# Zero blocks copied within DRAM instead of stored from SBUF, with the freed SBUF holding an eleventh weight chunk

## Chip, cores, metric

One core of a Trainium2 chip. The metric is device time in microseconds (us) of one execution. A run counts as slow when it lies more than 1.5% above the fastest run of the same kernel; verdicts use the fast runs alone.

## The reference, cut to what matters

A decode step of two attention layers (A) and two MLP layers (B), forward and backward. The outputs are the result and the gradients of all inputs and weights but one.

```python
def _A_ref(x, k_cache, v_cache, wq, wo):         # D=1024, 32 heads of 128, 4 groups, Sk=32768
    W = min(4096, max(256, Sk // 4))             # only the last 4096 positions are attended to
    k = k_cache[:, :, Sk - W:, :]; v = v_cache[:, :, Sk - W:, :]
    ...
    return o @ wo
x = x + A(norm(x)); x = x + B(norm(x)); x = x + A(norm(x)); x = x + B(norm(x))
_out, _vjp = jax.vjp(...)                        # out_2, out_3: gradients of k_cache and v_cache
```

The gradients of the two caches, out_2 and out_3, are zero at the first 28,672 of 32,768 positions of each group. These zeros are 58.7 MB, and the kernel has to write them.

## The kernel before

A tile of zeros in SBUF (4 KB per partition) is stored 112 times, 128 rows of 4 KB each. Some of these stores go out on the SP queue. The others go out on the GpSimd queue behind a "gate": a tiny copy that reads a tile of the computation, so that the zeros start only when that tile is there.

```python
NB = 6                       # buffers of the ring "strm" for streamed weights
NR = 10                      # wo chunks kept in SBUF, of 16
...
strm = ctx.enter_context(tc.tile_pool(name="strm", bufs=NB))
...
ZC = 2048
zt = keep.tile([P, ZC], BF16, name="zt")
nc.gpsimd.memset(zt[:], 0.0)
# zero_jobs: 112 destinations of 128 rows x 4 KB in out_2 and out_3  (loop cut)
def zeros(n):
    for _ in range(min(n, len(zero_jobs))):
        nc.sync.dma_start(zero_jobs.pop(0), zt[:])
def bg_zeros(n, after):
    if n:
        nc.gpsimd.tensor_copy(gate_t[:], after[:, 0:1])
    for _ in range(min(n, len(zero_jobs))):
        nc.gpsimd.dma_start(zero_jobs.pop(0), zt[:])
...
def w1_load(i):              # wo_load and w2_load take ring buffers in the same way
    w = strm.tile([P, F // 2], BF16, name="w1_c", tag="st", padded_shape=[P, 2048])
    nc.sync.dma_start(w[:], w1_v[:, t, hf * (F // 2):(hf + 1) * (F // 2)])
    return w
...
def w1_T():                  # the last pass over w1: 16 streamed loads
    i, ws = w1s["n"], w1s["ws"]
    w = w1_load(i); ws[i] = w
    if i in Z["W1m"]:        # 2, 5, 8, 11, 13
        bg_zeros(1, ws[i - 1])          # the gate reads a ring buffer
    xpose(...)
...
zeros(Z["A1d"])              # 23 blocks on the SP queue, after the last attention stage's loads
```

Of the kernel before, what the change touches and what calls it, by code (L numbers as in the profile page):

```python
# [9 lines left out]
BF16 = mybir.dt.bfloat16  # L10
# [4 lines left out]
P = 128  # L15
# [1 line left out]
DH = 128  # L17
G = 4
NB = 6
NR = 10  # L20


@with_exitstack
def kernel(
# [22 lines left out]
    nc = tc.nc  # L47
# [20 lines left out]
    keep = ctx.enter_context(tc.tile_pool(name="keep", bufs=1))  # L68
# [44 lines left out]
    ident_f = keep.tile([P, P], FP32, name="ident_f")  # L113
    make_identity(nc, ident_f[:])
    nc.vector.tensor_add(sel2[:], ident_f[:, 0:P:64], ident_f[:, 32:P:64])
    ZC = 2048
    zt = keep.tile([P, ZC], BF16, name="zt")
    nc.gpsimd.memset(zt[:], 0.0)

    zero_jobs = []  # L120
    per = ZR // P * DH
    for out_t in (out_2, out_3):
        for g in range(G):
            zflat = out_t[0, g, 0:ZR, :].rearrange("(p r) d -> p (r d)", p=P)
            for i in range(per // ZC):
                zero_jobs.append(zflat[:, i * ZC:(i + 1) * ZC])

    def zeros(n):
        for _ in range(min(n, len(zero_jobs))):
            nc.sync.dma_start(zero_jobs.pop(0), zt[:])  # L130

    gate_t = keep.tile([P, 1], BF16, name="gate_t")

    def bg_zeros(n, after):

        if n:
            nc.gpsimd.tensor_copy(gate_t[:], after[:, 0:1])
        for _ in range(min(n, len(zero_jobs))):
            nc.gpsimd.dma_start(zero_jobs.pop(0), zt[:])  # L139

    ev = [0.0, 0.0]

# [191 lines left out]
    wq_t = [wq_b[:, t, hf, :] for t in range(TD) for hf in range(2)]  # L334
    wo_b = keep.tile([P, NR, 2, D], BF16, name="wo_b")
    wo_kept = {c: wo_b[:, c, :, :] for c in range(NR)}
    wo_rows = wo_b[:].rearrange("p c t d -> p (c t) d")

    def load_kv(pool, nm, src):
        kv[nm] = pool.tile([P, G, TK, DH], BF16, name=nm)  # L340
        for g in range(G):
            nc.sync.dma_start(kv[nm][:, g, :, :], src[g])
# [7 lines left out]
    def wo_load(c):  # L350
        if c < NR:
            w = wo_kept[c]
        else:
            w = strm.tile([P, 2, D], BF16, name="wo_c", tag="st")[:]
        nc.sync.dma_start(w, wo_v[c])
        return w
# [83 lines left out]
    def attn_fwd(x_col, lname, first):  # L440
        if first:
# [4 lines left out]
            load_kv(keep, "V", v_v)  # L446
            for c in range(NR):
                wo_load(c)
# [22 lines left out]
        if not first:  # L471
            for c in range(NR, min(NO, NR + NB)):
                held[c] = wo_load(c)
            bg_zeros(Z["A3"], n_bf)
            for w in wq_t:
                xq["wq"].extend(w[:, k * 1024:(k + 1) * 1024] for k in range(2))
            fill(1, ["wq"], "v")
# [69 lines left out]
        NRW = NO - 2 if first else NO - 3  # L547
        late, early = list(range(NR, NO)), list(range(NR))
        order = early + late if first else late[0:3] + early + late[3:]
# [62 lines left out]
    class W2Pass:  # L612
# [33 lines left out]
        def rest(self, done, g_bf, x_col, xname, gbc, zn, last=None):  # L646
            for c in range(NW2):
                w = self.get(c)
                if c >= done:
                    self.fwd(c)  # L650
                    self.tc(c)
                scr = work.tile([P, D], BF16, name="scr", tag="kp")
                nc.vector.tensor_tensor_reduce(out=scr[:], in0=w[:, 0, :], in1=gbc[:], scale=1.0, scalar=0.0,  # L653
                                               op0=ALU.mult, op1=ALU.add, accum_out=self.wg[:, c, 0:1])
                if c:
                    self.bwd(c - 1, g_bf)
                if c in zn:
                    bg_zeros(zn[c], self.wg[:, c, :])
            hook("w1")
            self.bwd(NW2 - 1, g_bf)  # L660
            hook("w1b")
            if last is not None:
                last()
            x_new = keep.tile([P, TD], FP32, name=xname)
            nc.vector.tensor_add(x_new[:], x_col[:], self.acc.cols(0, TD))
            nc.vector.tensor_copy(self.wg[:, :, 1:2], self.acc.cols(TD, TD + NW2)[:, :, None])
            return x_new, self.wg

    def mlp_fwd(x_col, lname, g_bf):
# [5 lines left out]
        for i in range(2 * TD):  # L675
            t, hf = i // 2, i % 2
            w = w1_load(i)
            if i == 0:
                bg_zeros(Z["B2a"], x_col)
            if i == 4:  # L680
                gbc = bcast_row(g_bf)
            for b in range(NW2):
                fb = hf * NW2 + b
                o = (b // 2) * 2 * P + b % 2
                mv(hacc, fb, w[:, o:o + 2 * P - 1:2], n_bf[:, t:t + 1], False, t == TD - 1)
# [131 lines left out]
    def attn_bwd(g_col, g_bf, lname, sv, first, nxt):  # L817
# [63 lines left out]
        if first:  # L881
            pre.extend(w2_load(c) for c in range(NB))
            bg_zeros(Z["A3d"], g_bf)
            fill(100, ["V"])
        else:
            after_stream()
            zeros(Z["A1d"])
# [406 lines left out]
    for at in (27, 33):  # L1294
        jobs.insert(at, lambda: zeros(2))
    run(1000)
    zeros(1000)
    assert not zero_jobs

# [29 lines left out]
```

## Time and profile before

| | before |
|---|---|
| median (range), first three runs | 442.62 us (442.41 to 445.55) |
| span of the profiled run | 439.8 us |
| packet time: all packet records added up, over 16 engines | 436.4 us |
| rest of the span | 3.3 us |

The packet time is the useful summary here. Added up, the packets take 436.4 of 439.8 us, so the kernel can only gain by moving fewer bytes or moving them faster, and it loses whatever makes the packets longer or leaves the engines empty. The two rows are a summary and not exact: packet records overlap a little (full stretches show a DMA share of 1.02 or 1.03 below), so the rest understates the time in which engines stand empty. Counted from the trace, as the share of the 16 engines with no packet under way at each moment, the empty time is 13.4 us.

The prediction shows the main rows of the page. In such rows each digit is the busy share, in tenths, of one of 40 equal slices of the span. PE is TensorE, PEld its weight loads, DVE VectorE, ACT ScalarE, POOL GpSimd, SP SyncE (a "q" marks the part that issues); L139 is line 139 of the kernel. One more row, the bytes moved in each of the 40 slices (11 us each):

```profile
GB/s 319 421 422 414 407 409 391 409 380 373 407 416 354 353 349 352 409 395 416 415 409 376 401 388 362 363 401 414 417 415 418 416 380 267 379 401 409 417 421 304
```

It stays near 410 wherever large blocks move, be they zeros or weights. The dips to 350 (slices 13 to 16) are stages with many small packets.

### The profile page before, as it was taken

To read this page: it belongs to the slowest core of one execution; us is meant where nothing else is said; L and a number is where in the kernel's file an instruction comes from. 1 tells how busy PE (TensorE), PEld (TensorE's weight loads), DVE (VectorE), ACT (ScalarE), POOL (GpSimd) and SP (SyncE) were. 2 spreads that over 40 slices of the span, in tenths; PEclk is the share of its full clock that TensorE was granted. 3 is DMA by queue.
4 is the path that set the end of the run, shared out by engine and by line. 5 is a ranking of instruction groups with operands and counts; after the bars stand their busy time and mean duration, and the time that the engine had idled before them with its cause. 6 is when DMAs were issued, how large, how long until landed. Compare 5 with 4: busy or idle time off the path is not lost.

```text
span 439.8 us, 11711 instructions
## 1 busy us (share of the span) xinstructions
PE 319.4 (73%) x5004; PEld 216.7 (49%) x5004; DVE 241.1 (55%) x494; ACT 219.4 (50%) x254; POOL 64.6 (15%) x168
## 2 busy tenths in 40 slices
PE   1566855597989988878897588777956688588830
PEld 0343525487467978866776588755421122211100
DVE  3134201186333757584357555365369889899930
ACT  1131200075153867666865243426047888798840
POOL 2000000011420322152332111214010010000000
PEclk9998565575879999998999558899975555555555
DMA  8999999999999999999999999999999996999997
GB/s 319 421 422 414 407 409 391 409 380 373 407 416 354 353 349 352 409 395 416 415 409 376 401 388 362 363 401 414 417 415 418 416 380 267 379 401 409 417 421 304
DMA packets 48721, 171.18 MB, mean 389 GB/s; under 512 B 4929, under 2 KB 12125, under 8 KB 44573
## 3 DMA queue, kind: packets, MB, share of 16 engines
q1 hardware_dynamic: 36208, 125.58, 72.8%
q0 software_dynamic: 12416, 44.84, 25.7%
q8 instruction: 39, 0.64, 0.5%
q14 instruction: 14, 0.11, 0.1%
q10 hardware_dynamic: 44, 0.01, 0.0%
HBM read 71.58 MB, written 98.84 MB: 388 GB/s over the span
## 4 chain that ended last, share of the span: by engine, by line
PE 24%; ACT 13%; DMA 10%; DVE 4%; issue 2%; POOL 1%; ACTq 0%; DVEq 0%; SPq 0%
DMA w_c<-in_B_w_dram 7%; PE tps L196 7%; PE ops L232 6%; PE acc L232 5%; ACT wq_b L149 3%; ACT K L149 3%; DMA out_dram<-wq_b 2%; ACT st_o L149 2%; PE sm L232 2%; ACT V L149 2%; ACT wo_b L149 2%; PE rw L995 1%; PE d L232 1%; PE tps L629 1%; PE wps L155 1%
## 5 line engine op out<-in xcount | busy, mean ns | idle before, releaser
L139 POOL DMA_DIRECT2D out_dram<-zt x85 | 45.6, 540 | 43.2 <-DMA out_dram<-zt 37.0
L232 PEld LDWEIGHTS <-w_c 128*128 128x128 bf16 x1120 | 37.9, 103 | 25.2 <-DMA w_c<-in_B_w_dram 19.0
L639 ACT COPY w_c<-tps 128x1024 bf16<-128x1024 bf16 x28 | 28.3, 1012 | 30.1 <-PE tps L629 22.4
L653 DVE CUSTOM_DVE_ANT_0 scr<-w_c,gbc 128x1024 bf16<-128x1024 bf16 x28 | 34.2, 1221 | 12.0 <-DMA w_c<-in_B_w_dram 10.8
L232 PE MATMUL ops<-V 2*128 2x512 bf16 (+1 forms) x160 | 33.4, 602 | 4.8 <-ACT V L149 1.2
L149 ACT CAST wq_b<-ops 128x1024 bf16<-128x1024 f32 (+1 forms) x33 | 35.9, 1126 | 1.9 <-PE ops L232 1.8
L146 DVE CAST wq_b<-ops 128x1024 bf16<-128x1024 f32 (+1 forms) x31 | 34.4, 1139 | 2.0 <-PE ops L232 1.6
L149 ACT COPY K<-tps 128x1024 bf16<-128x1024 bf16 x20 | 19.5, 1023 | 28.3 <-PE tps L196 28.2
L232 PEld LDWEIGHTS <-V 128*128 128x128 bf16 (+2 forms) x448 | 16.8, 102 | 33.7 <-issue 32.0
L232 PE MATMUL ops<-wo_b 2*128 2x512 bf16 x120 | 23.5, 553 | 10.0 <-ACT wq_b L149 2.8
L629 PE MATMUL tps<-ident_bf,w_c 128*128 128x128 bf16 x224 | 24.2, 275 | 0.7 <-DMA w_c<-in_B_w_dram 0.7
L232 PE MATMUL acc<-a_pair,w_c 128*128 128x16 bf16 x448 | 15.9, 173 | 9.5 <-DMA w_c<-in_B_w_dram 9.2
L149 ACT COPY w_b<-tps 128x1024 bf16<-128x1024 bf16 x20 | 19.5, 1015 | 5.3 <-PE tps L196 5.2
L196 PE MATMUL tps<-ident_bf,w_c 128*128 128x128 bf16 x224 | 19.0, 250 | 3.5 <-DMA w_c<-in_B_w_dram 3.4
L146 DVE COPY w_c<-tps 128x1024 bf16<-128x1024 bf16 (+1 forms) x20 | 12.7, 650 | 15.5 <-PE tps L196 13.4
L146 DVE COPY K<-tps 128x1024 bf16<-128x1024 bf16 x12 | 8.1, 689 | 23.6 <-PE tps L196 23.6
L232 PE MATMUL q<-wq_b,nA_pair 128*32 128x512 bf16 x128 | 9.5, 414 | 15.7 <-DMA wq_b<-in_A_wq_dram 15.7
L232 PEld LDWEIGHTS <-wo_b 2*128 2x128 bf16 (+1 forms) x184 | 7.4, 98 | 27.0 <-issue 24.7
L149 ACT CAST K<-ops 128x1024 bf16<-128x1024 f32 x17 | 17.1, 1012 | 6.3 <-PE ops L232 5.5
L196 PE MATMUL tps<-ident_bf,K 128*128 128x128 bf16 x256 | 20.0, 239 | 0.0
L146 DVE CAST K<-ops 128x1024 bf16<-128x1024 f32 x15 | 18.3, 1222 | 3.1 <-PE ops L232 2.7
L248 DVE COPY yr<-acc 128x512 f32<-128x512 f32 x6 | 4.2, 692 | 28.7 <-PE acc L232 28.7
(326 smaller groups left out, 657.5 us busy)
## 6 DMA issues: line engine op xcount, KB each, us to landing
out_dram<-zt POOLq DMA_DIRECT2D x85, 512.0 KB, 10.3
w_c<-in_B_w_dram SPq DMA_DIRECT2D x32, 448.0 KB, 6.7
w_c<-in_B_w_dram SPq DMA_DIRECT2D x28, 512.0 KB, 7.7
out_dram<-zt SPq DMA_DIRECT2D x27, 512.0 KB, 10.0
wo_c<-in_A_wo_dram SPq DMA_DIRECT2D x24, 512.0 KB, 8.3
wq_b<-in_A_wq_dram SPq DMA_DIRECT2D x8, 1024.0 KB, 21.1
out_dram<-K SPq DMA_DIRECT2D x8, 1024.0 KB, 9.6
out_dram<-wq_b SPq DMA_DIRECT2D x8, 1024.0 KB, 10.3
```

Of the source, the lines that this page charges most:

```text
L139: nc.gpsimd.dma_start(zero_jobs.pop(0), zt[:])
L146: nc.vector.tensor_copy(out_ap, in_ap)
L149: nc.scalar.copy(out_ap, in_ap)
L155: nc.tensor.matmul(ps, lhsT=ident_bf[:], rhs=ident_bf[:, None, :].to_broadcast([P, 4, P]), start=True, stop=True, skip_group_check=True)
L196: nc.tensor.transpose(ps[:, b, :], ap, ident_bf[:])
L232: nc.tensor.matmul(out_ap, lhsT=lhsT, rhs=rhs, start=start, stop=stop, skip_group_check=True, **kw)
L248: nc.vector.tensor_copy(yr[:], bank[:])
L629: nc.tensor.transpose(self.ps[c][:, b, :], w[:, 1, b * P:(b + 1) * P], ident_bf[:])
L639: nc.scalar.copy(self.w[c][:, 1, :], self.ps.pop(c)[:].rearrange("p b c -> p (b c)"))
L653: nc.vector.tensor_tensor_reduce(out=scr[:], in0=w[:, 0, :], in1=gbc[:], scale=1.0, scalar=0.0, op0=ALU.mult, op1=ALU.add, accum_out=self. ...
L995: nc.tensor.transpose(ps[:, j, :], sp[:, j, :], ident_bf[:])
```

## The change

Its intent: one zeroed block of out_2 becomes the source, and all other zero blocks are copied from it, from DRAM to DRAM, with rows of 8 KB instead of 4. The SBUF tile of zeros is no longer needed; its 4 KB per partition keep one more chunk of wo, which saves one 512 KB reload in each of three passes.

```diff
-NR = 10
+NR = 11
...
-    ZC = 2048
-    zt = keep.tile([P, ZC], BF16, name="zt")
-    nc.gpsimd.memset(zt[:], 0.0)
+    ZC = 4096
...
-                zero_jobs.append(zflat[:, i * ZC:(i + 1) * ZC])
+                for hp in range(2):
+                    zero_jobs.append(zflat[hp * 64:hp * 64 + 64, i * ZC:(i + 1) * ZC])
+    zsrc = zero_jobs[0]
+    def seed(tiles):
+        zero_jobs.pop(0)
+        for i, t in enumerate(tiles):
+            nc.gpsimd.memset(t[0:64, :], 0.0)
+            nc.gpsimd.dma_start(zsrc[:, i * 2048:(i + 1) * 2048], t[0:64, :])
...   (in zeros and in bg_zeros)
-            nc.sync.dma_start(zero_jobs.pop(0), zt[:])
+            nc.sync.dma_start(zero_jobs.pop(0), zsrc)
...
+    seed([wo_b[:, c, :, :].rearrange("p t d -> p (t d)") for c in (NR - 2, NR - 1)])
```

More of the change, by code (lines that the diff above doesn't have):

```diff
@@ L138, in bg_zeros @@
         for _ in range(min(n, len(zero_jobs))):
-            nc.gpsimd.dma_start(zero_jobs.pop(0), zt[:])
+            nc.gpsimd.dma_start(zero_jobs.pop(0), zsrc)
     ev = [0.0, 0.0]
```

## The prediction

> **What bounds the kernel now.** I first read the page's header, its 40 slices (11 us each), the HBM totals and the largest DMA groups.
>
> ```profile
> PE   1566855597989988878897588777956688588830
> DVE  3134201186333757584357555365369889899930
> DMA  8999999999999999999999999999999996999997
> HBM read 71.58 MB, written 98.84 MB: 388 GB/s over the span
> out_dram<-zt POOLq DMA_DIRECT2D x85, 512.0 KB, 10.3
> out_dram<-zt SPq DMA_DIRECT2D x27, 512.0 KB, 10.0
> wo_c<-in_A_wo_dram SPq DMA_DIRECT2D x24, 512.0 KB, 8.3
> ```
>
> The DMA row is 9 in all but four slices; no compute engine is near that before 320 us. 171 MB pass through the 16 DMA engines. Of these, 112 x 524,288 B = 58.7 MB are zeros for the parts of out_2 and out_3 outside the window: one third of all traffic. These are what the change touches.
>
> Next I asked for the busy time in stretches: two in which nearly nothing but zeros moves on the GpSimd queue, one with zeros on the SP queue, and the hole near the end.
>
> ```profile
> core 0: us, PE busy (x) PEld busy (x) DVE busy (x) ACT busy (x) POOL busy (x), PEclk, DMA share, GB/s
> 120.00:132.00 12.00, 9.92 (x224) 8.09 (x220) 5.10 (x16) 5.66 (x10) 3.20 (x6) 0.80 1.02 414
> 216.00:236.00 20.00, 19.73 (x351) 16.50 (x348) 11.85 (x22) 12.54 (x14) 7.71 (x14) 1.00 1.02 409
> 301.00:322.00 21.00, 18.18 (x253) 9.90 (x249) 7.45 (x20) 5.50 (x9) 1.56 (x10) 1.00 1.03 416
> 366.00:377.00 11.00, 8.77 (x60) 2.81 (x59) 10.71 (x17) 8.84 (x9) 0.00 (x0) 0.50 0.58 235
> ```
>
> Zeros alone keep the engines full at 409 to 416 GB/s. The only real hole is 366 to 377 us: 0.42 x 11 = about 5 us, where VectorE (10.71 of 11 us) sets the pace of the outputs. Only that much extra DMA time could hide.
>
> Last I followed the chain of work between 238 and 290 us.
>
> ```profile
> 240.61 10.60 DMA w_c<-in_B_w_dram
> 253.00 7.86 DMA w_c<-in_B_w_dram
> 272.20 7.44 DMA w_c<-in_B_w_dram
> 281.57 5.80 DMA w_c<-in_B_w_dram
> ```
>
> PE waits 6 to 11 us for weight loads right after a stretch of 28 zero blocks. Zeros aren't filling free time there: DMA time in front of a load is span. So I treat the kernel up to about 325 us as bound by the sum of DMA packet times, and the rest by VectorE, ScalarE and DMA in about equal parts.
>
> **What the Trainium skill says.**
> - "Perfetto Trace Analysis", DMA Optimizations: batching transfers into larger ones ("2KB → 4KB or 8KB") can help much. The trace agrees only weakly: its packet records have a median of 159 ns for 4096 B (zeros and loads alike) and 312 ns for 8192 B. Two small packets cost 318 ns, so 2% is to be had.
> - "HBM Reference", Specifications (TRN2): about 716 GB/s for the memory domain that two cores share. No run here shows this limit: the kernel never moves more than some 420 GB/s in reads plus writes.
> - "DMA: Bandwidth & Descriptors", Latency and other measured facts: copies of 128-row tiles between HBM tensors reach 207 to 214 GB/s "per direction" at harmless row pitches. The trace has no such copy, so it neither agrees nor disagrees. The page doesn't say if the copy was one DMA or passed through SBUF.
> - The same page, Queues, rings and completion order: an engine alternates between its queues packet by packet. The trace fits: in 200 to 215 us 4 KB zeros and 4 KB loads each have about half of the bytes.
>
> **The change part by part.**
>
> 1. *Reloads removed.* With 11 instead of 10 wo chunks kept, the first pass still loads 16; each of the three later passes reloads 5 instead of 6. Loads of wo fall from 34 to 31. One chunk is 524,288 / 4096 / 16 = 8 packets per engine, 8 x 159 ns = 1.27 us. Three are **-3.8 us**, all in DMA-bound stretches.
>
> 2. *Longer runs.* A zero block was 128 rows of 4 KB, 8 packets per engine, 1272 ns; it becomes 64 rows of 8 KB, 4 packets. If a packet from DRAM to DRAM costs what an 8 KB load or store does, a block takes 4 x 312 = 1248 ns. 111 x 24 ns = **-2.7 us**.
>
> 3. *Source moved from SBUF to HBM.* This is the term that decides. Every zero byte is now also read from HBM: 111 x 0.524 = 58.2 MB more reads, 129.8 - 1.6 = 128 MB in place of 71.6, and 227 MB of reads and writes together. In a zeros-only stretch at the old pace memory would have to serve 2 x 412 = 824 GB/s, above the page's 716. I cut the trace in 1 us slices from 40 us on: zeros are over 90% of the bytes in 90 of them and 40 to 90% in 65. Taking each slice's bytes with zeros counted twice, and stretching it where the demand passes a limit H, gives (an estimate): H 716: +13 us; 660: +23; 600: +37; 540: +57; 480: +85. [...] I choose H = 600: **+37 us**. About **-5 us** of that hides in the hole at 366 us or comes off because delayed zeros leave other stretches less crowded.
>
> 4. *Seed.* The block that served as SBUF source is written once through two kept wo chunks, 2 x 64 rows of 4 KB; it replaces a zero block, so it adds no bytes. It is early (two memsets of at most the old one's 1.81 us, then the DMA) and delays the wq loads by about 1.3 us, given back later because one block less is left. The two wo loads that follow wait for it only formally: they come near 40 us. 0.
>
> 5. *Compute.* Each backward pass drops one streamed chunk (one VectorE product of 1.22 us, eight transposes, one eviction) and gets 16 small matmuls on a kept one; the turn gets two more 8-block transposes with evictions of 0.7 to 1.0 us. A microsecond either way, set to 0. GpSimd's issue of 0.53 us is a third of a block's 1.27 us. The order of waits is unchanged: each zero DMA still waits only for the one eight before it in its queue; nothing serializes the copies on each other.
>
> Sum: 442.6 - 3.8 - 2.7 + 37 - 5 = **468 us**.
>
> **Rivals.**
>
> *A. The DMA engine alone sets the packet time, and memory keeps up.* For it: the packet medians (140 ns for 3584 B, 159 and 312 for the larger) lie on 6 ns + bytes / 26.8 GB/s, loads and stores alike, so the engine's own stream is the limit today. Then 3 is zero: 442.6 - 6.5 = 436, perhaps 437 as the last 100 us are half compute: **437 us**, -1.3%, no verdict of faster. This surely is what the author intends. Against it: 824 GB/s.
>
> *B. A DRAM-to-DRAM packet passes one shared path twice.* Then 8 KB takes about 624 ns, half rate, which is what 214 GB/s per direction would be. 444 packets per engine x 312 ns = +138 us; less 5 hidden: 442.6 - 6.5 + 133 = **570 us**. For it: 2 x 214 = 428, suspiciously near the 420 that the engines reach here. Against it: if the page's copies went through SBUF, 428 is only the known engine rate again, and loads and stores mix here without slowing one another.
>
> *C. Priority.* Where both queues are full, an engine now moves 8 KB of zeros for each 4 KB of weights, so the loads' share falls from 1/2 to 1/3: a 512 KB load beside zeros takes 8 x (159 + 312) = 3.8 us instead of 2.5. With fixed numbers of blocks this mostly moves waits: +0 to 4 us, on top of any other case. One shared 512 KB source read by all engines could also crowd a few memory banks; nothing here speaks for or against that, and it would look like B.
>
> **Range and chances.** I give A 0.36, a memory limit between A and B (447 to 545) 0.29, and B 0.35. My number is in the middle case, near the median of the whole; the outcome is two-peaked, so the range must span both: 434 to 578. Faster than 2% (under 433.8) needs 2.3 us more than A's sum can find: 0.04. Within 2%: 0.32. Slower: 0.64.
>
> **What will show it.** The changed page should list 20 streamed wo loads, 111 copies of out_dram from out_dram, HBM reads near 128 MB and writes still 98.8. The packet times decide: 8 KB copies near 312 ns mean A; 360 to 500 in zeros-only stretches but near 312 beside loads mean a memory limit; about 620 everywhere mean B. In A, GB/s in those stretches stays near 416; in B it halves with the DMA row still at 9, and waits for w_c after 240 us double. I am wrong altogether if copies are near 312 ns and the span still grows (then C or the new order of staging buffers), or if waits of zero DMAs on each other appear on GpSimd's queue.

## The result, and the profile after

| | before | after |
|---|---|---|
| median (range), 4 runs each | 444.09 us (442.41 to 446.92) | 461.87 us (459.49 to 463.74) |
| ratio of fast runs, 95% interval | | 1.0391 (1.0311 to 1.0471): slower |
| span of the profiled run | 439.8 us | 457.7 us |
| packet time over 16 engines | 436.4 us | 446.1 us |
| rest of the span | 3.3 us | 11.7 us |

Every ratio here is the mean time of one kernel's fast runs over the mean of the other's fast runs in the same rounds, so not quite the ratio of the medians quoted.

Recomputed from the listed runs this gives the recorded ratio within 0.15% everywhere but in one place: x_ring, where it gives 1.0136 and the record has 1.0213 (see there).

The last two rows of the table already divide the loss, roughly: of 17.9 us of span, 9.7 are packets that take longer and 8.4 are rest (with rounding). The prediction had foreseen the first part alone. The empty time counted from the trace grows less, from 13.4 to 19.7 us, but its places tell more: in the one MLP stage that is looked at below it grows from 1.0 to 10.0 us, and in the hole near the end it shrinks from 5.4 to 1.0.

From the page of the kernel after, the same rows as were shown of before, and the bytes moved:

```profile
PE   0455855578888989877993577678977578678830
DVE  3124101377325757742745454235429979899940
DMA  8999999999999999999999999579999999999997
GB/s 307 427 420 415 407 408 390 407 386 345 376 341 351 374 371 369 407 402 408 325 331 367 386 352 330 193 284 372 328 335 312 420 416 412 379 404 406 420 419 323
...
HBM read 128.20 MB, written 98.84 MB: 496 GB/s over the span
...
out_dram<-out_dram POOLq DMA_DIRECT2D x85, 512.0 KB, 12.2
...
out_dram<-out_dram SPq DMA_DIRECT2D x26, 512.0 KB, 12.7
wo_c<-in_A_wo_dram SPq DMA_DIRECT2D x20, 512.0 KB, 9.6
```

The counts are those predicted: 111 copies, 20 streamed wo loads, 128.2 MB read. Two things have changed in the rows. First, slices with nearly only zeros fall from about 412 to between 312 and 335 GB/s while the DMA row stays at 9 (slices 20, 21 and 29 to 31, counted from 1): the engines are occupied, but each packet takes longer. Second, the DMA row has a hole, "57" in slices 26 and 27 (286 to 309 us), where no zeros-only stretch lies.

The same in the busy times by stretch of the kernel after (the columns after the engines are the granted clock, the DMA share and GB/s):

```profile
core 0: us, PE busy (x) PEld busy (x) DVE busy (x) ACT busy (x) POOL busy (x), PEclk, DMA share, GB/s
220.00:240.00 20.00, 19.67 (x363) 16.32 (x361) 12.05 (x23) 12.44 (x14) 6.48 (x13) 1.00 0.99 329
280.00:308.00 28.00, 19.34 (x299) 17.93 (x300) 8.61 (x17) 6.81 (x8) 2.29 (x7) 0.62 0.71 253
320.00:340.00 20.00, 17.48 (x231) 9.32 (x229) 6.83 (x19) 4.33 (x8) 1.47 (x10) 0.97 0.99 331
```

The first and third are the zeros-only stretches that ran at 409 and 416 GB/s before; now they run at 329 and 331 with a full DMA share. The packet records of the copies agree: in 125 to 140, 220 to 240 and 320 to 340 us an 8 KB packet takes 384 to 392 ns in the mean, beside weight loads (187 to 208 and 250 to 300 us) 322 to 344. Two 4 KB packets of before took 2 x 164 = 328 ns in the mean.

The second stretch is the other kind: DMA share 0.71. It is the last pass over w1. The chain of waits of the kernel after shows who waits there:

```profile
263.75 6.67 DMA w_c<-in_B_w_dram
...
273.54 6.42 DMA w_c<-in_B_w_dram
...
281.37 4.97 DMA w_c<-in_B_w_dram
...
289.94 3.59 DMA w_c<-in_B_w_dram
...
295.69 0.33 SPq L373
296.07 5.39 DMA w_c<-in_B_w_dram
```

Before, the chain had its last such wait at 281.57 us. Now there are waits for weights right up to the end of the pass, although the DMA engines are idle a good part of the time, so the loads are *issued* late. At 295.69 the chain passes through the SP queue itself (line 373 is the issue of a w1 load): a load that was not issued before a buffer came free.

The stages' ends confirm where the loss is. Between the writing of the gradient ahead of this MLP's backward part and the one after it, before takes 233.4 to 291.6 us (58.2), after takes 236.0 to 308.2 (72.2): 14.0 of the 17.9 us.

The mark that the prediction named for copies serialized on each other, waits of zero DMAs on GpSimd's queue, is there in both kernels and grows from 37.0 to 45.5 us in all. In the waits of that queue (us in total, times, longest), first before, then after:

```profile
POOL out_dram L139 <- DMA out_dram<-zt: 37.0, 34, 2.1
```
```profile
POOL out_dram L145 <- DMA out_dram<-out_dram: 45.5, 35, 2.3
```

As many waits as before, none over 2.3 us: it is the same queue of eight, at a slower rate.

### The late loads

The addresses in the two built programs tell why loads come late. For every streamed load I counted how many loads back the previous user of its buffer lies. Before: 6 for every load of the kernel, the six buffers in turn. After: 6 everywhere except in the last pass over w1 and the wo loads behind it:

```
              w1 loads 0 ... 15                       wo loads
before   6 6 6 6 6 6 6 6 6 6 6 6 6  6  6  6        6  6 6 6 6  6
after    6 6 6 6 6 6 6 5 5 4 4 3 3  2 13 11        3 10 4 4 10
```

Load 13 takes the buffer of load 11, so it can be issued only when chunk 11 has been used: by then the pass runs with two buffers instead of six. The missing ones are those of loads 1, 4, 7 and 10, which come back last. Those are the tiles that the gates of the zero blocks read (`ws[i - 1]` for i = 2, 5, 8, 11). The counts are from the built programs, which no profile shows; the list LAST in b_bad below writes out the same order. So my theory after the result had two parts: **(a)** copies that move alone meet a limit on memory traffic, **(b)** the build hands out ring buffers in another order, and that is the hole. The rivals: rows of 8 KB crowd out loads; copies go through a path of half the rate everywhere; one shared source crowds a few memory banks; the hole comes from the zeros' arrival and not from the buffers.

### The profile page after: what moved, and what is told of

Read it like the earlier page. It is cut to its first block, busy times and chain, and to the rows that moved or that the text cites. A ratio compares the mean times of both kernels' runs of the same rounds, so it can differ in the third digit from the quotient of the medians.

```text
span 457.7 us, 11727 instructions
## 1 busy us (share of the span) xinstructions
PE 325.7 (71%) x5020; PEld 221.4 (48%) x5020; DVE 237.6 (52%) x488; ACT 220.8 (48%) x256; POOL 64.6 (14%) x171
## 4 chain that ended last, share of the span: by engine, by line
PE 23%; ACT 13%; DMA 12%; DVE 4%; issue 3%; POOL 1%; ACTq 0%; SPq 0%; DVEq 0%
DMA w_c<-in_B_w_dram 10%; PE tps L202 6%; PE ops L238 6%; ACT K L155 4%; PE acc L238 4%; ACT wq_b L155 3%; DMA out_dram<-wq_b 2%; PE sm L238 2%; ACT wo_b L155 2%; ACT st_o L155 2%; PE rw L1002 2%; ACT V L155 1%; PE wps L161 1%; PE d L238 1%; DVE wo_b L152 1%
## 5 line engine op out<-in xcount | busy, mean ns | idle before, releaser
L238 PEld LDWEIGHTS <-w_c 128*128 128x128 bf16 x1120 | 38.0, 104 | 30.7 <-DMA w_c<-in_B_w_dram 24.8
L145 POOL DMA_DIRECT2D out_dram<-out_dram x85 | 42.5, 503 | 52.7 <-DMA out_dram<-out_dram 45.5
L202 PE MATMUL tps<-ident_bf,w_c 128*128 128x128 bf16 x224 | 21.2, 267 | 10.1 <-DMA w_c<-in_B_w_dram 10.0
L636 PE MATMUL tps<-ident_bf,w_c 128*128 128x128 bf16 x224 | 23.5, 270 | 0.7 <-DMA w_c<-in_B_w_dram 0.7
L202 PEld LDWEIGHTS <-w_c 128*128 128x128 bf16 x224 | 17.8, 122 | 10.9 <-DMA w_c<-in_B_w_dram 10.9
L155 ACT COPY w_c<-tps 128x768 bf16<-128x768 bf16 (+1 forms) x12 | 10.0, 834 | 26.9 <-PE tps L202 26.9
L238 PEld LDWEIGHTS <-wo_b 2*128 2x128 bf16 (+1 forms) x232 | 8.8, 99 | 27.6 <-issue 25.4
```

The costliest lines, as they stand in the source:

```text
L145: nc.gpsimd.dma_start(zero_jobs.pop(0), zsrc)
L155: nc.scalar.copy(out_ap, in_ap)
L202: nc.tensor.transpose(ps[:, b, :], ap, ident_bf[:])
L238: nc.tensor.matmul(out_ap, lhsT=lhsT, rhs=rhs, start=start, stop=stop, skip_group_check=True, **kw)
L636: nc.tensor.transpose(self.ps[c][:, b, :], w[:, 1, b * P:(b + 1) * P], ident_bf[:])
```

## The experiments

Single profiles of one kernel differ by some us in the engines' empty time, so the packet times and the ratios are given side by side. All packet times and rests below are of one profiled run. The profiled runs of before (441.54 us), after (459.49) and x_ring (448.37) are each faster than the runs taken with them.

| run | ratio to before (95%) | packet time, us | rest, us |
|---|---|---|---|
| after | 1.0391 (1.0311 to 1.0471) | 446.1 | 11.7 |
| x_ring (ratio: see its section) | 1.0213 (1.0142 to 1.0284) | 444.3 | 2.3 |
| x_gate | 1.0265 (1.0194 to 1.0336) | 450.6 | 5.9 |
| b_bad (profiled run slow) | 1.0188 (1.0127 to 1.0249) | 440.7 | 18.0 |
| x_ring_nr10 | 1.0304 (1.0235 to 1.0372) | 451.1 | 4.6 |
| x_ring_4k | 1.0244 (1.0183 to 1.0304) | 448.6 | 5.4 |
| c_alone | 1.0291 (1.0225 to 1.0358) | 454.2 | 3.4 |
| c_beside | 1.0133 (1.0058 to 1.0208) | 437.0 | 10.2 |
| b_seed | 1.0016 (0.9990 to 1.0043) | 437.0 | 8.5 |
| mix | 1.0155 (1.0104 to 1.0205) | 435.9 | 12.4 |
| b_nb5 | 1.0340 (1.0303 to 1.0376) | 440.9 | 17.9 |

All of these gave the right result. Two further runs, m_copy and m_share, move data only and are wrong on purpose.

### x_ring: the changed kernel, the six buffers in strict turn

```diff
-    strm = ctx.enter_context(tc.tile_pool(name="strm", bufs=NB))
+    strm_pool = ctx.enter_context(tc.tile_pool(name="strm", bufs=1))
+    class Ring:                  # used as strm
+        n = -1
+        def tile(self, shape, dtype, name, tag, **kw):
+            self.n += 1
+            return strm_pool.tile(shape, dtype, name=name, tag=f"st{self.n % NB}", **kw)
```

> The changed kernel with one difference: the six streamed-weight buffers are taken in strict turn (six tags of one buffer each), where the build of the changed kernel gives the last pass over w1 buffers back after 5, 4, 3 and 2 loads. Theory T (two costs: copies share a memory limit in stretches of zeros alone, about 14 to 17 us; the buffer order of that pass adds 6 to 8 us of holes): 454 us, 451 to 457, and the DMA row between 280 and 310 us is back near 9. Rival R (the holes come from 8 KB copies crowding out the loads, buffers don't matter): 460 to 463, holes stay.

Measured: 452.70 us median; one of the four runs (457.08) is marked slow. The recorded ratio 1.0213 doesn't leave it out, though: it is what the three runs other than the profiled one (453.44, 451.96, 457.08) give. The three runs marked fast (448.37, 453.44, 451.96) give 1.0136. So x_ring costs 1.4 to 2.1% over before, and what is read from its ratio is uncertain by that much. To see the hole go, the DMA row around the end of that pass, in 40 slices of 1.1 us that end 4 us after the pass does; first before (251.6 to 295.6 us), then after (268 to 312), then x_ring (258.4 to 302.4):

```profile
DMA  9999999998999999999779999999979999999999
```
```profile
DMA  8999999988898988970676960089998006999789
```
```profile
DMA  9999899969999999999997999999999999999999
```

Zeros and sixes in the kernel after are slices in which engines stood empty; with the strict turn they are gone, and the rest of the span falls from 11.7 to 2.3 us (the empty time of this stage from 10.0 to 1.1). The stage takes 62.8 us (after: 72.2; before: 58.2). What remains of x_ring's loss is packet time, 444.3 against 436.4. Part (b) is worth about 1.0391 - 1.0213 = 1.8% or 8 us by the recorded ratios (2.5% or 11 us with x_ring at 1.0136), and the two ratios are of different rounds.

### b_bad: the kernel before, with the buffer order of after

```diff
+    LAST = (0, 1, 2, 3, 4, 5, 0, 2, 3, 5, 0, 3, 5, 3, 1, 4, 3, 2, 1, 4, 0, 5)
...  (Ring as above, but loads 76 to 97 take the buffers that LAST lists)
+        tag=f"st{(4 + LAST[self.n - 76]) % NB if 76 <= self.n < 98 else self.n % NB}"
```

> The kernel before, zeros from SBUF, with the buffer order of the changed kernel forced on the last pass over w1 (reuse after 6, then 5, 5, 4, 4, 3, 3, 2 loads). Theory T: 4 to 8 us slower than before, 447 to 451, with holes in the DMA row between 265 and 290 us. Rival R: 442 to 445, no difference.

Measured: 456.44 us median, 1.0188 by the two fast runs (452.76 and 453.32). The other two (459.56 and 460.45) count as slow, the first by a hair; with them the ratio would be larger. No copy is in this kernel, so the order alone costs 8 us (0.0188 x 445). The class Ring shows no cost by itself: b_seed has it too. Its page has the same hole in the same place:

```profile
DMA  7999999999998999999999997679999997799997
```

That page is of a slow run, so only the hole's place is read from it, not its size. With x_ring, this shows (b) from both sides.

### x_gate: the changed kernel, the gates read another tile

```diff
+    n_gate = pair_col("gB", "B4", TD)          # a small tile, ready long before
...
-            bg_zeros(1, ws[i - 1])
+            bg_zeros(1, n_gate)
```

> The changed kernel with one edit: the five GpSimd gate copies of the last pass over w1 read a small tile that is ready long before, in place of a streamed w1 tile. Nothing else of the ring is touched, and in the build every streamed buffer is again reused after exactly 6 loads, as in the kernel before. Theory (the gates' reads hold four of the six buffers in the changed build, and that costs the hole between 280 and 312 us): DMA row 9 throughout there, time like that of the kernel with the strict turn, ratio 1.015 to 1.03 to the kernel before (the copies stay). Rival 1 (the hole comes from the gates' zeros arriving between the loads, not from the buffers): these five blocks now arrive earlier and the hole or the waits for w_c stay, ratio 1.035 to 1.045.

Measured: in the build, with the original ring, every buffer is again reused after exactly 6 loads. So it is the gates' reads that take the four buffers out of turn. The time is 457.18 us median, ratio 1.0265: inside what the theory expected and below the rival's 1.035 to 1.045. Its DMA row has one 8 left of the hole:

```profile
DMA  8999999999999999999999999899999999899997
```

The five blocks now go out together near the start of the pass (issued at 271.7 to 274.7 us; in after one by one from 272.5 to 296.5), and the stage still takes 239.0 to 308.3 us (69.3): its empty time falls from 10.0 to 3.5 us, but the packet time of the run rises to 450.6. In this profile removing the gates repairs less than the strict turn does; by the ratios (1.0265 and 1.0213) the difference lies inside the intervals.

### x_ring_nr10: the copies without the eleventh chunk

```diff
-NR = 11
+NR = 10        # on top of x_ring
```

> Copies from DRAM and buffers in turn, but 10 kept wo chunks as before: what the eleventh chunk is worth beside x_ring. If the three reloads lie in DMA-bound stretches, 3 to 4.5 us slower than x_ring (about 458). If they are hidden: within 1 us of x_ring. Against before it then holds the copies alone.

Measured: 457.39 us, ratio 1.0304, in the same rounds as x_ring. The copies, with the longer rows, cost 3.0% or 13.5 us. The eleventh chunk gains 1.0304 - 1.0213 = 0.9% or 4 us by the recorded ratios, and nearer 7 us with x_ring's runs marked fast (packet times: 451.1 - 444.3 = 6.8). The two intervals overlap, so 4 to 7 us is an estimate and not a settled figure.

### m_copy: the rate of copies by themselves

Six phases of DMAs on one queue and no computation: stores from SBUF into rows with the gradient's pitch, stores into contiguous rows, copies from one block, copies from many blocks, copies from one contiguous block, and copies beside loads.

> Wrong results on purpose: nothing but DMAs, in phases on the SP queue: 28 stores of a 512 KB zero block from SBUF in rows 56 KB apart, 28 stores to contiguous blocks, 22 copies from one source with rows 56 KB apart, 20 copies from 20 sources, 18 copies from one contiguous source to contiguous blocks, 12 copies beside loads. Theory T (a limit on reads plus writes of the memory, near 660 GB/s): stores 410 to 418 GB/s, all three kinds of copies alike at 320 to 345. Rival H (the one shared source crowds a few banks): one source 320 to 345, 20 sources or contiguous ones at 380 to 416. Rival B (an engine passes a copied byte twice): 205 to 220 in all copies.

Measured, in the order of the first five phases (columns at the end: DMA share, GB/s):

```profile
20.00:45.00 25.00, 0.00 (x0) 0.00 (x0) 1.00 1.03 420
50.00:85.00 35.00, 0.00 (x0) 0.00 (x0) 1.00 1.03 420
95.00:118.00 23.00, 0.00 (x0) 0.00 (x0) 1.00 0.99 336
128.00:150.00 22.00, 0.00 (x0) 0.00 (x0) 1.00 1.00 330
160.00:178.00 18.00, 0.00 (x0) 0.00 (x0) 1.00 1.01 337
```

Copies move 330 to 337 GB/s, a fifth less than stores and far from half: the half-rate path of rival B falls. One source is not slower than many (336 and 330), and the pitch does not matter (337, although the contiguous blocks became packets of 32 KB): no crowding of banks is seen. Counted as reads plus writes, 330 to 337 are 660 to 674 GB/s. The sixth phase failed: its loads waited for nothing and ran at the very start, so it says nothing about copies beside loads.

### m_share: copies mixed with loads and stores

One queue, in turn: load and store; copy and load; two copies and a load; copy and store; copies alone. This repairs the failed phase.

> Wrong results on purpose, DMAs alone, all on the SP queue, in 512 KB blocks: 8 stores; 14 loads and 14 stores in turn; 14 copies and 14 loads in turn; 10 times two copies and a load; 12 copies and 12 stores in turn; 10 copies. With a limit near 660 GB/s on reads plus writes: loads with stores at 410 to 416 GB/s, one copy to one load 400 to 412 (demand 618), two to one 380 to 400 (demand 687), copies alone 320 to 340. If the copy itself is slow in an engine, not the memory: one to one gives 365 to 375 (the mean of 412 and 332), two to one 350 to 360.

Measured, the first four phases:

```profile
25.00:45.00 20.00, 0.00 (x0) 0.00 (x0) 1.00 1.03 419
55.00:80.00 25.00, 0.00 (x0) 0.00 (x0) 1.00 1.02 421
92.00:120.00 28.00, 0.00 (x0) 0.00 (x0) 1.00 1.01 392
132.00:152.00 20.00, 0.00 (x0) 0.00 (x0) 1.00 1.02 423
```

Copy and load one to one run at the full 421 GB/s. If a copied packet were slow in the engine itself, 421 and 333 would mix to 2 / (1/421 + 1/333) = 372. As a sum of reads and writes the phase moves 1.5 x 421 = 632 GB/s. Two copies to one load: 392 x 5/3 = 653. So the limit is on that sum, at 653 to 674, and it binds only where copies are the larger part of the traffic (about 0.6 or more: 421 x 1.6 = 674). This is part (a), and it is the prediction's "memory limit" case, with the limit higher than chosen. Whether the memory itself or the way to it sets the limit isn't shown. (The fifth phase's 302 GB/s runs into the end of the program and isn't used.)

### c_alone and c_beside: which copies cost

The kernel before with some of the blocks copied: in c_alone the 65 that move with little beside them (stages A3, A3d and A1d), in c_beside 43 others, which go out beside weight loads. Both keep the zero tile, ten chunks, and rows of 4 KB, and have the strict turn and a seed through two wo chunks; the last three blocks are stored from SBUF in both.

```diff
-            bg_zeros(Z["A3d"], g_bf)
+            bg_zeros(Z["A3d"], g_bf, True)     # True: in c_alone copied, in c_beside stored from SBUF
```

> The kernel before (10 kept chunks, the SBUF zero tile, buffers in turn) with only the 65 blocks copied within DRAM, in rows of 4 KB, that move while nothing is loaded (14 at the start of the third stage, 28 and 23 in the two attention backward passes); the other 46 are stored from SBUF as before. Theory T (copies cost only where they are alone): nearly the whole price of the copies, 2.4 to 3.6% over before, 455 to 460 us. Rival R (copies cost beside loads, by crowding them): within 1% of before.

> The complement: only the 43 blocks that move beside weight loads are copied within DRAM, 65 come from SBUF. Theory T: within 1% of before, 443 to 448. Rival R: 2 to 3% slower, 454 to 458. If both this and the other are near 1.5%, copies cost the same everywhere.

Measured: c_alone 456.15 us, ratio 1.0291, nearly the whole cost of all copies; c_beside 449.06 us, ratio 1.0133. The stretches, first c_alone, then c_beside:

```profile
125.00:140.00 15.00, 11.97 (x271) 8.76 (x268) 4.22 (x13) 5.26 (x10) 3.04 (x6) 0.77 1.00 317
220.00:240.00 20.00, 18.38 (x308) 15.28 (x311) 9.42 (x14) 16.32 (x20) 6.21 (x12) 1.00 1.02 347
```
```profile
125.00:140.00 15.00, 12.52 (x269) 9.03 (x270) 4.34 (x14) 5.89 (x11) 2.99 (x6) 0.77 1.01 390
220.00:240.00 20.00, 19.72 (x350) 16.50 (x348) 11.84 (x22) 12.56 (x14) 8.08 (x16) 1.00 1.03 415
```

c_alone's packet time grows by 17.8 us (454.2), c_beside's by 0.6 (437.0): copies beside loads are free for the DMA engines, as m_share says. Yet c_beside is 1.3% slower where I had expected less than 1% (the interval, 0.6 to 2.1%, allows it), and the two halves add up to 4.2%, more than the 3.0% of all copies in x_ring_nr10. So some of either cost may not lie in the copies. The profiled run of c_beside shows 10.2 us of rest, but b_seed shows 8.5 at a cost of 0.2%, so that is no explanation. One stretch stands out, 145 to 160 us: DMA share 0.81 (before 1.02, b_seed 0.98), with PE busy for all 15 us at a granted clock of 0.88 (1.00 in both others); one profile can't say why. **What makes c_beside slower stays open.**

### x_ring_4k: rows of 4 KB instead of 8

```diff
-    ZC = 4096
+    ZC = 2048       # on top of x_ring: 128 rows of 4 KB, no halves
```

> Copies and buffers in turn as in x_ring, but in 128 rows of 4 KB instead of 64 of 8 KB: the run length by itself. By packet times 111 blocks x 24 ns = 2.7 us slower where copies are not memory-bound, so 0 to 2 us slower than x_ring. If the larger packet's priority beside the loads hurts (rival C of the prediction), 2 to 5 us faster than x_ring.

Measured: 454.27 us, ratio 1.0244 against x_ring's 1.0213 (or 1.0136) of other rounds. Rival C wanted the 4 KB rows to be faster, because 8 KB of zeros would no longer stand against each 4 KB of weights. They are not: they seem 0.3% slower by the recorded ratios, which is within the intervals and near what the longer rows were predicted to bring.

### b_seed: the seed alone

```diff
+    seed_to = zero_jobs.pop(0)
+    for i in range(2):
+        nc.gpsimd.dma_start(seed_to[64 * i:64 * i + 64, :], zt[64 * i:64 * i + 64, :])
```

> The kernel before with one thing of the change: the first zero block is written at the very start, in two halves of 64 rows, beside the first loads (buffers in turn, which the build of the kernel before has anyway). All other blocks come from the SBUF tile as before. If the seed delays the first stage and isn't given back: 1 to 2.5 us slower (0.3 to 0.5%), and the first gate over 1 us later. If the block left out later pays it back, as the prediction put it: within 0.2% of before.

Measured over 22 runs, three of them slow: 446.47 us, ratio 1.0016, interval from 0.999 to 1.0043. No cost is shown, and none over 0.4%. This tests the extra early store alone: it comes from the zero tile, so the memsets of two wo chunks, and the wo loads that wait for them, are not in it.

### mix and b_nb5: could a version beat both?

mix copies only beside loads and stores the blocks that move alone from a ring buffer that is zeroed for the occasion; it keeps eleven chunks. b_nb5 has no copy at all and pays for the eleventh chunk with the sixth ring buffer.

```diff
+        z = strm.tile([P, 2048], BF16, name="z_sb", tag="st")       # mix
+        nc.gpsimd.memset(z[:], 0.0)
...
-NB = 6                                                              # b_nb5
-NR = 10
+NB = 5
+NR = 11
```

> A version that should beat both if T holds: 11 kept wo chunks, 4 KB rows, buffers in turn; the 71 blocks that move alone are stored from a zeroed buffer of the streamed ring (one of six is free when five wo chunks are streamed), only the 40 others are copied within DRAM. Three reloads less and no memory limit: 0.5 to 1.2% faster than before, 438 to 442. If the buffer held for zeros delays the w2 loads after the first attention backward pass: 442 to 447. If R holds, above 450.

> No copies at all: the 4 KB for the eleventh wo chunk are taken from the streamed ring (five buffers instead of six), the zero tile stays. The reloads saved are worth 0.9%. If five buffers keep the loads as far ahead as the engines need: 0.5 to 1% faster than before, 440 to 442, which would beat both kernels. If the sixth buffer is needed: 0 to 2% slower.

Measured: mix 450.34 us, ratio 1.0155; b_nb5 459.69 us, ratio 1.0340. I had hoped for less than 1 in both, and both miss. The packet time of mix is the lowest of all (435.9), so the bytes are saved, but 12.4 us of rest eat it up; that the zeros hold a ring buffer meanwhile is the likely reason, argued and not tested. The waits of the SP queue show the hold but not its price (line 383 issues a w2 load):

```profile
SPq L383 <- DMA out_dram<-z_sb: 45.2, 3, 38.8
```

The kernel before has a like wait, of 35.3 us for VectorE, at its w2 loads. b_nb5 shows what fewer buffers cost: with five the rest is 17.9 us. The sixth buffer is worth more than the eleventh chunk. No version tried here beats the kernel before.

## Why the prediction was right or wrong

The verdict (slower) and the range hold, and 468 us is 6 us from 461.87. But a range of 434 to 578 left little room to miss, and the sum came out well by luck in part: two errors have opposite signs.

1. **Item 1, reloads removed (-3.8): right in sign.** x_ring_nr10 against x_ring gives 4 to 7 us, not resolved.
2. **Item 2, longer runs (-2.7): not contradicted.** x_ring_4k was about 1.5 us (0.3%) slower by the recorded ratios, unresolved.
3. **Item 3, source in HBM (+37): right mechanism, wrong size.** The limit is on reads plus writes, and packets become longer only in zeros-only stretches, as the prediction's own mark for that case said (384 to 392 ns there, 322 to 344 beside loads). The mis-sized term is H, chosen as 600 GB/s without a measurement. The runs give 653 to 674. The prediction's table has +23 at 660; less the 5 hidden and item 2's 2.7, that is +15, and x_ring_nr10 measures +13.5. With H = 660 the sum would have been 454 us; x_ring, the change without the buffer effect, has 452.70. The -5 us that were to hide in the hole near the end did: its empty time falls from 5.4 to 1.0 us.
4. **Item 4, seed (0): right as far as tested** (b_seed, +0.16% with zero in the interval; without the memsets of the wo chunks).
5. **Item 5, "The order of waits is unchanged": wrong.** It holds for the zero DMAs, each behind the one eight before it, but not for the weight loads. The order of the instructions had been looked at, and how the build assigns the ring's buffers had not. It cost about 8 us: +1.9% in b_bad, and -1.8% (to -2.5%) when undone in x_ring. The closing sentence of the prediction did name "the new order of staging buffers" as a way to be wrong, but no term of the sum had it.

So 442.6 - 3.8 - 2.7 + 23 - 5 + 8 = 462 us is the sum with both corrections, put together after the result.

Small misreadings that moved no term: the DMA row before has three slices below 9, not four; PE is at 9 in six slices before 320 us, so a compute engine is near; GpSimd's issue of 0.53 us is two fifths of 1.27, not a third.

**The rivals.** A (the engine alone, 437) falls by the 330 GB/s of copies alone. It would be right for copies beside an equal amount of loads. B (half rate, 570) falls by the same number: copies move 330, not 210. C (priority) isn't seen in x_ring_4k. The crowded source falls by 336 against 330 in m_copy. A prediction with a chance of 0.35 on B had given too much weight to a figure for copies of another shape.

**Open:** why c_beside costs 1.3%; how much of x_ring's loss is left over after the copies and the chunk, given its two ratios; and why the build holds the gates' buffers longer once zeros are copied: that it does, and that the gates' reads are the condition, is in the built programs; what in its rule makes the difference isn't known.

## What to carry to other kernels

In these runs a DRAM-to-DRAM copy counted twice, as a read and as a write: in a stretch where little else moved it ran at the limit on their sum (330 instead of 420 GB/s), while beside an equal amount of loads it cost the DMA engines nothing (421). In a kernel bound by DMA, adding bytes to memory traffic in order to free SBUF needs that comparison stretch by stretch, with the limit measured by a small kernel of DMAs alone. And when a change touches what reads a ring of buffers, compare the buffers' turn in the two builds, not just the instructions' order: a pass that silently drops from six buffers to two shows as empty DMA engines with waits for loads at the same time.

## What the Trainium skill lacked or had wrong

- "DMA: Bandwidth & Descriptors", Latency and other measured facts: the only rate for copies between HBM tensors is that of the row-pitch entry (214 GB/s per direction, called full). Here 64 rows of 8 KB copied alone move 330 to 337 GB/s per direction, with a row pitch of 57,344 B or contiguous alike (m_copy). The page's shape was not run.
- "Perfetto Trace Analysis", Roofline (under Engine Utilization): it says that one core alone is bounded by its 16 DMA engines, at about 435 GB/s. That fits loads and stores (419 and 420), but not copies within DRAM: they stop at 330 to 337 with all engines occupied (m_copy). The page makes no exception for copies.
- "HBM Reference", Specifications (TRN2): it gives about 716 GB/s per domain and about 425 for one core that streams alone, but not whether reads and writes share the 716, nor what one core reaches when it does both. Here one core reached 653 to 674 GB/s of reads plus writes, and mixes that stay under it ran at the full engine rate (copy and load, 632 GB/s in the sum, 421 of DMA traffic: m_share).
- "Perfetto Trace Analysis", DMA Optimizations: its example goes from 2 KB to "4KB or 8KB" and doesn't say what the last step adds. Here it adds little: two 4 KB packets take 318 ns and one of 8 KB 312 (medians), and x_ring_4k and x_ring differ by 0.3%, unresolved.
- No page warns that a pool may hand out a ring's buffers out of turn. Here it cost 1.9% (b_bad), visible only in the built program and as a hole in the DMA row.
